# A new stored order for all tasks of a fused attention and ReGLU kernel on one core

## The chip, the cores and the metric

The kernel runs on one core of a Trainium2 chip. The metric is the device time of one execution in microseconds (us). PE stands for TensorE's matmuls and PEld for its weight loads, DVE for VectorE, ACT for ScalarE, POOL for GpSimd, and SP for SyncE, which only issues transfers here.

## The reference

Attention over 8 batches of 8 heads, 576 positions of 64 elements, with 16 beacon keys and values that every position sees ahead of the causal ones; then a feed-forward layer over all 8 x 576 = 4608 rows.

```python
k_all = concatenate([beacon_k, k]); v_all = concatenate([beacon_v, v])
scores = q @ k_all.T / 8, causal behind the 16 beacon columns
a = softmax(scores)
x = (a @ v_all), heads side by side      # 4608 x 512
out = (relu(x @ w_gate) * (x @ w_val)) @ w_out   # 512 -> 1536 -> 512
```

Inputs and the output are float32; the kernel computes in bfloat16 with float32 sums.

## The kernel before

The work of a batch is cut into small tasks. Loads bring a block of q, k or v in float32 into one of eight staging tiles `st`; a cast on POOL (some on DVE) rounds it to bfloat16 (L542 for q and k, L497 for v); PE transposes q and k blocks against an identity (L553, L626); ACT or DVE copies them out of PSUM into `qT` and `kT` (L493, L495). Score products (L824) go to PSUM, DVE adds the mask and takes the row minimum (L772), ACT takes the exponential with its sum (L779), DVE the reciprocal (L785), and POOL multiplies the row by it (L790). The results stand in `pb` (four tiles) and, for the last few positions of each head, in `pa` (two tiles). From batch 1 on a DMA transpose on SP's queue turns them into `pTb` and `pTa` (L910, 28 and 6 of them); for batch 0, and for one `pa` more, PE does this (L900). Products with v (L920 for `pTb`, L943 for `pTa`) give x, which is copied into the resident `xT`.

The feed-forward layer takes `xT` in ten spans of columns (240, 336, seven of 512, 448). For each of 12 hidden blocks PE makes four gate and four value matmuls (L981, L986), ACT applies the ReLU (L992), DVE multiplies (L997) into `hT`; then twelve matmuls for each 128 rows make the output (L1012), which is copied to one of three tiles `osb` and stored (L1026). All three weights stay in SBUF. PE fills its early waits with matmuls on the mask that nobody reads (L1064, "fillers").

The 2399 tasks are made in a fixed manner and numbered in the order in which they are made. A string `ORDER` (L77 on) lists them in the order in which their instructions are emitted; this order fixes each engine's instruction list, and SP's queue of transfers too. An entry is a task's number, with a letter where the engine is chosen (`a` ACT, `v` DVE, `g` POOL), and behind a colon the numbers of the tiles or PSUM banks that it takes. `f7:7` is a filler of seven matmuls on bank 7. Nothing is decided at run time: each engine goes through its list in order, and an instruction waits where data or a tile's previous use is not done. So a task that waits holds up all behind it on its engine, and a DMA transpose that waits for POOL holds up the loads and stores behind it on SP's queue.

```python
for t in plan.replay(ORDER):
    t.run(t)
```

The tasks that the prediction names, by number and the line of their work:

| tasks | engine | what |
|---|---|---|
| 431 | PE | scores, L824, batch 0 |
| 14.74 us row of L824 (469) | PE | scores, batch 0 |
| 1420, 1421, 1422 | POOL, SP, PE | the `pa` chain of one batch: L790, transpose L910, product L943 |
| 1282, 1279, 1306, 1305, 1294, 1316 | POOL | L790 on `pb`, other parts |
| 331, 338 | POOL | casts of loads, L542 |
| 1177 | SP | a `pTb` transpose, L910 |
| 1124, 1140, 1159, 1161, 1175 | POOL | L790 on `pb` |
| 285, 287 / 319 | POOL | casts of q, k loads, L542 / of a v load, L497 |
| 2065 | PE | a value group of four matmuls, L986 |

Of the kernel before, what the change touches and what calls it, by code (L numbers as in the profile page):

```python
# [80 lines left out]
420 59v:2 486:5.6.0.1 475 430 472 63v:0 454 473 438 487 64:2 453 435 60:7 464 69v 439 491 452 440:4 61a 72:0 476 495:3.1 13 73 441v:0 492 f3:7 455 465  # L81
496 488 444:0 467 f2:7 16 65v 504:4.5 497 77:1 489 500 442:2 445a:0 458 f3:7 505 457 f1:7 501 466 513:6.0 493 456 509 446:3 506 477 f1:7 f3:7 502 498
468 514 447a 443a 15 478:3 510 71v 482:4 518 522:1.2 515 19 511 524 479a:0 523:5.6 67g 516 519 483v:0 480:3 512 528 484:4 481a 18 525 548:7.3.2.3 485v
529 549 90:5 494 557:1.2 91 1734:4 553 17 550 1738:0 562 1735:0 566:5.6 507 503 1739:1 f2:7 558 563 1736:4 508 567 1742:7 559 490 1737:0 554 526 520
499 1740:4 571 1743:2 575:1.0 81:3 568 517 1741:1 82 1744:2 576 86:4 572 584:3.4 527 f1:7 580 1746:5 577 521 532:7 569 530 560 586 1747:1 531 536:1
533a:0 1748:5 1745:2 534:6 74:1.1 1749:3 537a 540:2 564 535v 587 78:2.1 95:0 544:5 542:1 541v:1 125:7 538:6 581 570 588 573 585:2.3 551 565 543a 555
539v 1750:0 561 545v 610:6.7.0 590 1751:1 552 546:4 589 578 611 591 1754:0 579 75:5 612 1752:1 1755:0 582 592 547v 76a 1756:3 574 613 1758:2 1757:5
593 594:4 1753:4 1759:0 596:5 556 595v:2 598:1 1762:0 583 614 79:7 597v 1760:4 1763:1 615 599a 602:2 1761:6 80a 606:5 87:1 616:1 604:4 617v:0 83:0
600:3 603v:3 92:2 101:3 84:6 601a 88:7 113:4 605v 607a 93:0 96:0 618:3 105:1 85a 89v 20 109:2 608:2 94a 99:6 97:5 126:1.0 609v 1766:1 98a 1764:4 619a
127:6 620:0.2.0.1 102:2 1765:7 128a 635:3.5 1770:7 1767:2 621 21 643 103:6 628 1768:4 622 1771:0 106:0 104a 1772:1 1769:8 624 1774:7 114:2 1773:9  # L90
1778:4 629 623 123:4 1776:1 1775:1 644 1779:2 1780:6 121:5 110:1 631 1792:4 1777:10 133:1 636 630 650:7.0 137:2 1781:11 1793:0 1787:2 637 129:0 645
646 659 107:6 652 639 111:4 1782:1 632 625 638 647 651 649 108a 112v 115:3 1788 633 653 640 116v 627 654 665:6.5 658 626 674:3.4 634 661 666 1794:7
642 660 670 1783 667 100:1 655 676 671 657 1784 119:6 124 677 700:0.6.2.3 1795:12 1785a:0 122 141:4 1796:5 701 679 117:3 668 656 708 715:7.1 702 678
648 1789 134:1 709 1797:1 704 669 717 145:1 1800:4 176:5 662 1790a:1 1798:3 716 664 723 703 1802:5 663 718 1799:13 641 1801:2 1804:2 724 1786 120 711
675:3.4 672 705 680 1803:14 149:6 1805:0 681 1806:0 726 683 682 1808:2 719 1807:15 673 690:3 1812:5 710 1809:1 712 130:0.0 730:6.0 684 725 1810:7 720
732 686 713 1814:1 738 1813:2 721 731 685 714 1816:5 1811:8 118 131:2 739 734 1818:4 687 1815:1 1817:1 689 745:3.7 733 1819:2 1820:1 688 741 735 746
754:5.6 132a 736 695:1 740 1822:4 750 722 1821:1 1824:0 757 142:0 747 1823:11 1828:1 151:7 707 751 756 755:3.4 138:2 1825:2 727 1832:2 742 748 758 737
763 1826:7 706 1829:0 752 749 1830:0 759 152 1827:4 728 691:1 760 764 693:7 762 692a 1831:5 765 761 780:5.6.1 694v 139:1 781 135:0 753 1833:1 770:2
143:3 766 1836:7 140v 146:1 136a 1834:2 782 729 1837:2 767 147:4 144a 1835:6 1838:0 769 783 148v 744 696:1 698:2 784 1839:10 790:5.6.0.1 785 805:4.7
1840:3 792 160:1 768 791 786:0 799 743 794 1841 177:2.1 775:3 798 697a 813 793 1842 150:0 787v:1 699a 814 801 153:0 788:2 807 800 178:1 1843a:2  # L100
820:0.5 789v 161:2 773:6 179a 828 815 806 771:2 1845:3 795 829 809 156:0 821 808 772v 1846 164:1 816 822 180:7 774v 831 835:2.4 1847 823 840 830 1791
824 817 1850:6 832 172:6 833 841 825 836 170:3 826 844:0.1 1848a:0 819 778:5 810 846 837 834 776:7 1851 811 777a 838 847 796 779a 157:1 154:2 849
845:4.5 184:0 165:0 848 1852 853 839 188:1 192:2 166:3 802 155v 1853a:1 804 162:0 1849 158:7 1855:1 854 812 174:5 850 167v 855 173 168:4 1857:6 163v
852 1856:2 159v 1859:2 827 856 797 857 1858:8 870:7.0.2.3 1860:1 851 885:4.3 1863:5 871 893 872 185:2 860:2 1867:2 886 874 878 842 894 843 1861:6 873
887 1864:2 858 896 1865:7 1862:9 803 1868:0 171 879 1871:5 895 859 888 875 1866:10 818 880 900:6.1 889 169 1869:2 865:1 909 881 175 901 1875:3 908
1872:1 189:0.1 1870:11 911 915:7.4 181:1 902 1873:2 910 890 916 904 892 903 182:1 876 1879:0 183v 193:1 1876:2 210:7 1874:4 917 861:6 863:3 196:2 897
882 862a 912 920 202:6 924:1.2 1880:0 200:1 925:6.7 927 921 1877:5 918 905 926 919 864a 226:0 1881:0 877 1878:13 928 933 914 950:3.4.0 929 868:5 206:5
906 1844 934 866:1 1883:2 930 224:4 867v 935 931 1882:14 1854 186:1 891 1884:1 190:6 187v 1887:0 203:0 191a 951 936 907 194:2 1885:6 932 195a 937 952
197:2 1888:2 940:2 1889:7 1886:15 953 899 869v 1895:1 938 954 1890:0 198:3 207:1 204:0 1891:4 199a 883 205v 884 959:6.5.7.2.0.1 1892:0 939 208:3 218:6
913 961 1893:4 898 209a 220:2 973 211:2 960 1899:0 965 1894:1 955 964 962 1897:3 974 956:0 1896:1 1900:2 963 1901:6 1898:2 967 230:5 941:0 975 943:4  # L110
# [56 lines left out]
2327 2334:12 2322 2351:7 2317 2328 2342:7 2338:13 2349:5 2348:1 2353:0 2329a:1 2343:2 2330 2318 2344:0 2352:2 2363:4 2319a:0 2354:1 2345:3 2320 2355:2  # L167
2346:5 2350:0 2323 2356:0 2364:2 2359:3 2365:0 2360:1 2324a:1 2357:2 2325 2367:7 2358:2 2361:3 2366:4 2368:0 2369:0 2371:4 2370:8 2373:2 2362:3 2372:1
2375:1 2374:10 2377:3 2376:2 2379:6 2378:9 2380 2384:0 2385 2381 2386 2382a:0 2389:5 2383 2387a:1 2388 2390 2391 2394:4.6 2392a:2 2393 2397:1 2395v:0
2398 2396  # L170
"""


# [924 lines left out]
```

## Time and profile before

| | |
|---|---|
| median of 3 runs | 400.01 us (399.12 to 400.79) |
| the profiled execution, its time | 399.52 us |
| the profiled execution, its span from first to last instruction | 397.6 us |
| granted PE clock over the span | 0.999 |
| HBM read, written | 38.54 MB, 9.44 MB |

A profile's page counts an engine's busy time as the union of its instructions; a PE that is busy need not be at its peak, since a matmul's start-to-start time is shorter than its duration. The chain is followed back from the last instruction, at each step to whatever released it. A releaser in square brackets, as in "[1.40 <-DMA pTa<-pa]", gives the idle time of that engine just before the row and what ended it. For a transfer the row of SP's queue is its issue; "DMA to landing" is the time from the issue to the last byte's arrival, as minimum, median and maximum.

### The profile page before, as it was taken

The page shows a single profiled execution, that of the slowest core. Times are in us where ns is not written, and L with a number is a line of the kernel's source. Part 1 is how long each engine was busy: PE and PEld are TensorE (multiplying, and loading weights), DVE is VectorE, ACT ScalarE, POOL GpSimd, SP SyncE. Part 2 cuts the span into 40 slices and gives each one's busy share as a digit, 9 for nine tenths or more (in the row PEclk, how much of TensorE's full clock was granted, in tenths as well). Part 3 has the DMA queues.
Part 4 walks back from the last instruction along what each step waited for, and adds up shares of the span by engine and source line. Part 5 has one row for each costly group of instructions (what it writes and reads, how often), then busy time and mean ns, then how long its engine had stood idle before and what let it go on. Part 6 is the DMA issues. An engine that isn't in the chain of part 4 may idle for free.

```text
span 397.6 us, 10026 instructions
## 1 busy us (share of the span) xinstructions
PE 380.1 (96%) x3384; PEld 199.7 (50%) x3428; DVE 274.2 (69%) x1008; ACT 270.3 (68%) x842; POOL 231.0 (58%) x447
## 2 busy tenths in 40 slices
PE   5789999999999999999999899999999999999996
PEld 3557855655454455454444454445444445444453
DVE  5899799888976888877876778567946832331230
ACT  1899699897877687789777789688746731332322
POOL 3799779959785789268827787663853650000000
PEclk9999999999999999999999999999999999999999
DMA  7999999999999999968997999988897556001102
GB/s 183 218 181 237 193 230 235 195 230 236 215 234 205 313 177 203 181 186 177 202 205 215 197 202 198 209 162 167 169 180 161 101 105 168 28 0 54 54 26 94
DMA packets 184100, 68.89 MB, mean 173 GB/s; under 512 B 158384, under 2 KB 179504, under 8 KB 184048
## 3 DMA queue, kind: packets, MB, share of 16 engines
q1 hardware_dynamic: 179216, 63.46, 74.5%
q0 software_dynamic: 4752, 4.72, 7.3%
q8 instruction: 27, 0.44, 0.5%
q14 instruction: 25, 0.20, 0.1%
q10 hardware_dynamic: 80, 0.07, 0.1%
HBM read 38.54 MB, written 9.44 MB: 121 GB/s over the span
## 4 chain that ended last, share of the span: by engine, by line
PE 83%; DMA 3%; issue 1%; DVE 1%; POOL 0%; ACT 0%; DVEq 0%
PE f L1012 22%; PE f L986 22%; PE f L981 22%; PE f L824 6%; PE f L920 6%; PE f L553 2%; DMA pTb<-pb 2%; DMA pTa<-pa 2%; PE f L943 1%; PE f L626 1%; PE f L874 1%; DVE f L772 0%; PE f L900 0%; POOL pa L790 0%; DVE kT L495 0%
## 5 line engine op out<-in xcount | busy, mean ns | idle before, releaser
L790 POOL TENSOR_SCALAR pb<-pb,small 128x384 bf16<-128x384 bf16 (+8 forms) x272 | 142.1, 538 | 45.5 <-DVE small L785 43.9
L779 ACT ACTIVATE pb<-f,small 128x448 bf16<-128x448 f32 (+8 forms) x272 | 144.8, 551 | 24.5 <-DVE small L772 19.7
L772 DVE CUSTOM_DVE_ANT_0 f<-f,mask 128x64 f32<-128x64 f32 (+8 forms) x288 | 136.3, 507 | 20.1 <-PE f L824 11.0
L997 DVE TENSOR_TENSOR hT<-g,f 128x512 bf16<-128x512 f32 (+3 forms) x120 | 74.4, 629 | 55.3 <-PE f L986 30.2
L981 PE MATMUL f<-xT,wg_r 128*128 128x512 bf16 (+3 forms) x466 | 108.1, 357 | 0.9 <-issue 0.2
L986 PE MATMUL f<-xT,wv_r 128*128 128x512 bf16 (+3 forms) x465 | 106.8, 357 | 1.2 <-issue 0.3
L1012 PE MATMUL f<-wo_r,hT 128*128 128x512 bf16 (+3 forms) x441 | 100.3, 374 | 1.5 <-issue 1.0
L992 ACT ACTIVATE g<-f 128x512 f32<-128x512 f32 (+3 forms) x120 | 65.8, 563 | 49.3 <-PE f L981 31.0
L981 PEld LDWEIGHTS <-wg_r 128*128 128x128 bf16 x480 | 45.0, 98 | 45.2 <-issue 2.5
L986 PEld LDWEIGHTS <-wv_r 128*128 128x128 bf16 x480 | 44.5, 98 | 44.2 <-issue 3.0
L1012 PEld LDWEIGHTS <-hT 128*128 128x128 bf16 (+3 forms) x456 | 41.9, 100 | 47.0 <-issue 2.9
L779 ACT ACTIVATION_READ_ACCUMULATOR pb<-f,small 128x1 f32 x272 | 60.0, 221 | 0.0
L542 POOL TENSOR_SCALAR h<-st 128x512 bf16<-128x512 f32 (+1 forms) x87 | 46.8, 547 | 22.5 <-DMA st<-in_q_dram 5.0
L772 DVE DVE_READ_ACCUMULATOR2_ANT small<- 128x1 f32 x296 | 41.2, 139 | 0.1
L824 PE MATMUL f<-kT,qT 64*64 64x64 bf16 (+7 forms) x640 | 34.6, 296 | 1.6 <-ACT pb L779 0.7
L497 POOL TENSOR_SCALAR v<-st 128x512 bf16<-128x512 f32 (+1 forms) x38 | 23.3, 616 | 19.7 <-DMA st<-in_v_dram 19.6
L493 ACT CAST xT<-f 128x240 bf16<-128x240 f32 (+2 forms) x46 | 16.1, 376 | 22.6 <-PE f L920 22.5
L785 DVE RECIPROCAL small<-small 128x2 f32<-128x2 f32 (+3 forms) x136 | 19.7, 160 | 12.0 <-ACT pb L779 10.8
L920 PE MATMUL f<-pTb,v 128*64 128x320 bf16 (+3 forms) x488 | 27.0, 254 | 0.4 <-DMA pTb<-pb 0.4
L824 PEld LDWEIGHTS <-qT 64*64 64x64 bf16 x640 | 14.7, 107 | 22.6 <-issue 17.7
L920 PEld LDWEIGHTS <-v 128*64 128x64 bf16 (+1 forms) x512 | 21.0, 109 | 9.9 <-issue 5.1
L553 PE MATMUL f<-ident,h 128*128 128x128 bf16 (+1 forms) x224 | 19.8, 222 | 5.7 <-DVE h L542 5.0
(62 smaller groups left out, 216.1 us busy)
## 6 DMA issues: line engine op xcount, KB each, us to landing
out_dram<-osb SPq DMA_DIRECT2D x34, 256.0 KB, 2.7
st<-in_k_dram SPq DMA_DIRECT2D x28, 256.0 KB, 4.6
st<-in_q_dram SPq DMA_DIRECT2D x28, 256.0 KB, 4.0
st<-in_v_dram SPq DMA_DIRECT2D x24, 256.0 KB, 4.6
st<-in_q_dram SPq DMA_DIRECT2D x16, 128.0 KB, 3.8
st<-in_k_dram SPq DMA_DIRECT2D x16, 128.0 KB, 4.1
st<-in_v_dram SPq DMA_DIRECT2D x8, 224.0 KB, 4.5
wv_r<-in_moe_w_val_dram POOLq DMA_DIRECT2D x3, 512.0 KB, 9.2
```

Of the source, the lines that this page charges most:

```text
L542: (nc.gpsimd if x.engine == "POOL" else nc.vector).tensor_scalar(to, src, by, 1.0, ALU.mult, ALU.mult)
L553: nc.tensor.matmul(to, h16.tile[:rows, a * P:(a + 1) * P], ident[:rows, :rows], start=True, stop=True)
L772: nc.vector.tensor_tensor_reduce(out=view(i, n - m), in0=view(i, n - m), in1=msk, scale=1.0, scalar=at(7) if m < n else 3.0e38, op0=ALU.ad ...
L779: nc.scalar.activation(ph.tile.rearrange("p a n -> p (a n)")[:, a:a + n], view(i), AF.Exp, bias=at(i), scale=-1.0, accum_out=at(4 + i))
L790: nc.gpsimd.tensor_scalar(one, one, at(8 + i), 1.0, ALU.mult, ALU.mult)
L824: nc.tensor.matmul(banks[k][b_].tile[64 * i:64 * i + 64, off:off + n], t.q.tile[r, 2 * g + i, 64 * j:64 * j + 64], t.kT.tile[r, 2 * g + i, ...
L920: nc.tensor.matmul(ps.tile[64 * hh:64 * hh + 64, d0:d0 + w], t.v.tile[:rows, c, D * h:D * h + D], rhs(64 * hh), start=(c == 0), stop=(c == ...
L981: nc.tensor.matmul(psg.tile[:, :mt], wg_r[:, ki, nf * P:(nf + 1) * P], xT[:, ki, m0:m0 + mt], start=(ki == 0), stop=(ki == KM - 1))
L986: nc.tensor.matmul(psv.tile[:, :mt], wv_r[:, ki, nf * P:(nf + 1) * P], xT[:, ki, m0:m0 + mt], start=(ki == 0), stop=(ki == KM - 1))
L992: r = add("ACT", c_act(mt), lambda _, psg=psg, g=g: nc.scalar.activation(g.tile[:, :mt], psg.tile[:, :mt], AF.Relu), (a,), (psg, g), -1000 ...
L997: hid.append(add("DVE", c_dve(mt), lambda _, psv=psv, g=g, nf=nf: nc.vector.tensor_mul(hT[nf].tile[:, :mt], g.tile[:, :mt], psv.tile[:, :m ...
L1012: nc.tensor.matmul(ps[c].tile[64 * c:64 * c + rows, :w], hT[nf].tile[:, t0:t0 + rows], wo_r[:, nf, w * c:w * c + w], start=(nf == 0), stop ...
```

## The change

Only the string `ORDER` differs. It holds the same 2399 tasks with another order, other tile and bank numbers, and another engine for 54 of the copies out of PSUM; its fillers are 13 entries with 43 matmuls in place of 14 with 46. The order on PE is much the same from about 30 us on: groups change places with neighbours. The orders on POOL, DVE and SP's queue change more. The head of the string, up to task 469:

```diff
-10 1 22:0 2 26:1 34:3 0 4 30:2 23v:0.0 8 38:4 24:0 9 5 f4:7 42:5 27g:1.0 7 25v 48:7 28:1 46:6 35v:0 31v:2 36:3 29v 32:2 50:0 f3:7 37v 33a 54:1 f2:7
-39v:1 410:4.5.0.0 58:2 11 431:6.0 6 40:1 411 43g:2 12 412 41a 423 44:2 413 45a 49g:0 422 3 436 414 448:3.1.0.0 62:7 415 421 f12:7 432 47g 426 68:5 450
-416 459 70:6 449 425 460 51g:0 451 469:2.4 424 66:4 f1:7 417 437 461 14 52:5 427 433 55v:1 470 53a 418 56:6 434 f8:7 474 428 463 419 57v 471 429 462
+11 4 22:0 3 2 26:1 34:3 0 5 1 30:2 f4:7 23v:0.0 9 38:4 8 12 24:0 42:5 27g:1.0 f2:7 48:7 28:1 35v:0 46:6 f2:7 6 29a 31v:2 f1:7 36:3 25v 32:2 50:0 f2:7
+37v 33a 39v:1 410:4.5.0.0 10 54:4 7 40:1 43g:2 411 423 58:2 413 41a 44:2 421 431:6.0 412 45a 49g:0 432 414 436 448:3.1.0.0 62:7 415 f7:7 422 416 47g
+68:5 460 424 451 469:2.4 425 70:6 461 51g:0 426 417 470 437 450 14 52:5 459 433 427 55v:1 53a 474 72:0 66:4 56:6 428 f3:7 449 464 429 434 57v 73 f7:7
...
```

Around transpose 1177, with the tasks on POOL that feed it (1124 to 1127, 1149 to 1151, 1168, 1169):

```diff
-1142 1123 1152 1972 1143 1266:0 1145 1144 1973 1146 1153 280:6 1147 1978 1974v:0 1155 1154 1981:3 1156 1975 1148 1979a:1 293:1 1162:0.1.5.6 1157 1980
-1096:7 1163 1098:4 318:2 1097a 1101:2 1158 1103:7 1170 1102a 1099a 1982 1136 1164 1104a 1140 1171 1166 1986:2 281:0.1 1165 1139 1267:4 1172 285:1
-282:1 1983 283v 1160 1268a 1167 1126 1187:7.0.4.5.2.3 1984a:2 1151 1995:1 1173 1189 1985 287:2 307:6 1201 1987 1188 1168 291:0 1190 1193 1203 300:7
-1125 1991:3 1191 1996:1 1127 1204 1192 1993:6 1194 1149 1202 1195 1150 1988 1174 1992:0 1169 1124 1205 1994:0 1999:7 1206 319:1 1177:3 1989v:0 1207
+1265 1977 1143 1124 271 1152 1972 1142 285:1 1146 1144 1973 287:2.1 1145 1153 1266:0 1147 1978 1154 1156 1981:3 1974v:0 1155 280:3 1157 1979v:1
+1162:0.1.5.6 1136 1096:7 291:0 1164 1101:2 1098:4 1097a 1158 1975 1171 1161 1103:7 1163 318:2 1099a 1982 307:6 1102v 1166 300:7 1170 281:0 1267:4 1165
+320:1 1148 1986:2 1127 1172 1167 1104v 1139 282:1 1268v 1173 1983 1160 283v 1168 1187:7.0.4.5.2.3 1984v:2 1149 1995:1 1125 1188 1985 1189 293:3 1169
+1991:3 1996:1 1174 1202 322:4 319:1 1192 1987 1175 1992:0 1201 1190 1193 1191 1993:6 1159 1150 1205 1204 1194 1988 1151 1206 1203 1994:0 1126 1195
+1999:7 1140 1177:3 1989v:0 1208 288:0.1 1196 1207 1214:3.2.4.6 2000:0 289v 294:1 1997:5 290a 1215 1216 2007:1 1209 1227 1218 1210 2003:0 1176 1219
```

Around the `pa` chain 1420, 1421, 1422 (316 and 337 are loads, 2048 and 1990 stores, 355 and 366 loads that come later in the new string):

```diff
-1416 1251:1 317 2040 1299 1254a 1252a 1417 1302 2041 1418 331:1 2046 327:0.0 1312 1317:0.1.5.6 2047a:2 1281 1313 1256:2 1319 1258:4 2042a:1 2048 1303
-1318 2054:3 1257a 1306 332:4 2043 1419 1325 1320 2049:7 337:0 339:2 1321 1326 328:2 2050 346:5 1291 1259v 1328 1294 1990 329v 315 1327 2055 355:6 1420
-1342:4.0.2.5.2.3 1314 1421:1 2063:6 1280 1343 1344 1304 2056 366:7 1316 2064:1 1357 353:3 1347 338:0 2051 1356 2057v:1 1360 1315 362:0 1348 2059:1
-1345 1305 1358 1361 1282 1322 2052v:0 2061:3 2060:0 1295 1359 1422:7 333:2 1346 2065:4 1323 2062:9 1349 1362 2067:2 1423v 1279 1363 1329 1324 2066:11
+1415:4.5.1 1253:0 330:5 1416 353:3 1251:1 2040 1309 337:0 1252a 1302 1254v 2041 1278 1417 1282 1418 2046 1281 2042v:1 1312 1317:0.1.5.6 2043 2047a:2
+1258:4 1313 1291 1303 1316 1318 1256:2 2054:3 315 1257a 1319 1326 2055 1320 1259v 338:0 1419 1325 1321 328:2 2049:7 331:1 329v 1327 1294 346:5 2050
+1279 332:4 1328 1306 1342:4.0.2.5.2.3 1305 2063:6 1343 1420 1356 1322 1344 2056 1323 1421:1 1347 1348 1324 2051 2057v:1 1280 362:0 1345 2059:1 1293
+1329 2052a:0 339:2 1357 2064:1 333:2 1346 2065:4 1361 1314 1359 1315 2061:3 1360 2060:0 1358 1304 1363 1422:7 1292 1332:0 2062:9 1350 2067:2 363:0
```

In the old string load 316 stands behind transpose 1255, in the new one ahead of transpose 1250, the one before it. The remaining lines of the string differ in the same manner.

More of the change, by code (lines that the diff above doesn't have):

```diff
@@ L82 @@
[L82 to L109, printed above, removed]
@@ new lines @@
+1843a:2 773:6 821 816 771:2 822 1845:3 809 828 156:5 179v 823 1846 164:1 808 829 1791 772a 774v 824 1847 172:6 815 825 180:7 830 835:2.4 817 795
+844:0.1 1848a:0 797 836 1850:6 831 153:0 840 837 1849 776:7 810 832 778:5 847 811 777a 157:1 841 154:2 846 1851 165:0 174:5 779a 848 170:3 158:7 812
+845:4.5 168:4 849 833 166:3 854 818 162:0 159a 1855:1 188:1 826 838 850 842 155a 853 827 1852 796 163v 1856:2 851 167a 1859:2 852 856 839 855 1857:1
+819 860:3 1860:1 857 885:4.3.2.3 1858:8 171 1853a:0 870:7.0 1867:2 872 843 1863:5 189:0.1 871 886 874 894 858 1861:6 887 873 1868:0 181:1 802 893
@@ L171 @@
+2350:0 2355:4 2324a:1 2353:0 2356:0 2352:2 2357:2 2354:1 2363:5 2359:3 2364:2 2367:7 2360:1 2319a:2 2365:0 2320 2361:3 2325 2366:4 2371:4 2362:3
+2369:0 2358:2 2372:1 2368:0 2373:2 2375:1 2374:10 2377:4 2370:8 2376:2 2379:6 2378:11 2384:0 2380 2381 2385 2382a:0 2383 2386 2389:5 2387a:1 2390 2388
+2391 2394:4.6 2392v:2 2393 2397:1 2395v:0 2398 2396
 """
```

122 lines of the change are left out of this document (71 added, 51 removed), and 6 rows, old and new, of the table ORDER.

## The prediction

> **What bounds the kernel now.** I read the page's span, busy times and chain first, then the busy time by stretch, then the waits one by one.
>
> ```profile
> span 397.6 us, 10026 instructions
> ...
> PE 380.1 (96%) x3384; PEld 199.7 (50%) x3428; DVE 274.2 (69%) x1008; ACT 270.3 (68%) x842; POOL 231.0 (58%) x447
> ...
> PE 83%; DMA 3%; issue 1%; DVE 1%; POOL 0%; ACT 0%; DVEq 0%
> ```
>
> PE is busy for 380.1 of 397.6 us and carries 83% of the chain, so at most 17.5 us can be won by any order, and only where PE stands still.
>
> ```profile
> 0.00:10.00 10.00, 5.33 (x45) 3.00 (x45) 5.75 (x42) 1.79 (x4) 3.60 (x15) 1.00 0.75 183
> 10.00:20.00 10.00, 7.91 (x75) 5.27 (x76) 8.96 (x51) 8.65 (x39) 8.00 (x17) 1.00 1.06 218
> 20.00:30.00 10.00, 8.56 (x100) 5.53 (x98) 10.00 (x38) 10.00 (x34) 9.88 (x20) 1.00 1.17 181
> ...
> 220.00:240.00 20.00, 18.44 (x218) 9.31 (x220) 16.12 (x55) 15.62 (x48) 15.91 (x31) 1.00 0.99 200
> ```
>
> The columns are the stretch, its length, the busy time of PE, PEld, DVE, ACT and POOL with their instructions, the granted clock, the DMA share and GB/s. In the first 30 us PE idles 4.67 + 2.09 + 1.44 = 8.2 us, and from 20 to 30 us DVE and ACT are full: there they bound the kernel, not PE. From 220 to 240 us PE loses 1.56 us. Two waits stand in the chain in order of time, both on a DMA transpose of softmax results:
>
> ```profile
> 112.50 7.62 DMA pTb<-pb
> ...
> 120.16 0.88 PE f L920 x16
> ...
> 215.53 6.25 DMA pTa<-pa
> ...
> 221.83 0.67 PE f L943 x20
> 222.50 0.87 PE f L986 x4
> ```
>
> PE's own idle before them is 0.4 us at 120.16 and 1.40 us at 221.83:
>
> ```profile
>   DMA pTb<-pb: 0.4, 1
> ```
>
> ```profile
> 221.83 0.67 PE L943 MATMUL f<-pTa,v 128*128 128x32 bf16 x20 [1.40 <-DMA pTa<-pa]
> ```
>
> So there are three prizes: the head, 0.4 us at 120, 1.4 us at 222. Everything else in this change can only keep PE fed or fail to.
>
> **The change, part by part.** The set of tasks stays the same; fillers go from 46 matmuls to 43, PE's instruction list from 6858 to 6852 rows, and 54 copies change engine (31 from ACT to DVE, 23 the other way).
>
> *Copies.* For the same 128x512 output copy:
>
> ```profile
> L493 ACT COPY osb<-f 128x512 f32<-128x512 f32 x24 | 14.0, 588 | 10.0 <-PE f L1012 9.8 <-ACT pb L779 0.2
> ...
> L495 DVE COPY osb<-f 128x512 f32<-128x512 f32 x10 | 6.9, 689 | 5.8 <-PE f L1012 4.5 <-DMA out_dram<-osb 1.3
> ```
>
> A net 8 copies on DVE cost some 8 x 0.1 = 0.8 us of engine time, hidden by the third of the span in which each of the two idles. If that cover were gone the whole 0.8 us would show; I take 0.
>
> *Head (tasks up to about 30 us).* Part of the constant and padding memsets move ahead of the first data, one 12-matmul filler becomes 7, and task 431 (a group of 256-column score products) moves behind two transposes.
>
> ```profile
> 9.03 0.25 DVE L463 MEMSET pb<- 128x32 uint32 x5
> ...
> 9.60 0.31 DVE L485 MEMSET xT<- 128x128 uint32 x2
> ...
> 11.05 0.43 DVE L772 CUSTOM_DVE_ANT_0 f<-f,mask 128x256 f32<-128x256 f32 x1
> ...
> 15.09 0.43 DVE L772 CUSTOM_DVE_ANT_0 f<-f,mask 128x256 f32<-128x256 f32 x1 [0.80 <-PE f L824]
> ```
>
> ```profile
> 12.06 2.74 PE L1064 MATMUL f<-mask,ident 128*128 128x256 bf16 x12
> 14.74 0.30 PE L824 MATMUL f<-kT,qT 64*64 64x256 bf16 x4
> ...
> 15.54 1.04 PE L1064 MATMUL f<-mask,ident 128*128 128x256 bf16 x8
> ```
>
> DVE is what the head waits for. On its list between 9 and 11.1 us stand memsets of about 0.6 us, of which about 0.3 stay behind: a gain of 0.3. Task 431's minima (the 11.05 row is one) can no longer start before about 11.3, since 431 now follows the second transpose, and DVE has then run out of other minima: I charge 0.5. The shorter filler (5 x 0.22 us less) lets the scores at 14.74 come about 1.1 us sooner, which removes most of DVE's 0.80 us wait at 15.09: a gain of 0.5. After that the two lists hold nearly the same DVE work up to 30 us. Sum -0.3; I take -0.2, with -1.1 (all of 0.3 and 0.80) and +0.5 (the loss alone) as ends. The three fewer fillers are inside this: they stand in time that DVE sets.
>
> Twelve fillers started over 2.68 us (12.06 to 14.74) and eight lasted 1.04, a spacing of 0.22 and about 0.11 us, though the granted clock reads 1.00 in this stretch. [...]
>
> *The wait at 222.* It is the chain of one task group: the normalisation of pa on POOL (task 1420, L790), its transpose on SP's queue (1421, L910), the product on PE (1422, L943). Three things move.
>
> ```profile
> 210.26 0.62 POOL L497 TENSOR_SCALAR v<-st 128x512 bf16<-128x512 f32 x1 [8.71 <-DMA st<-in_v_dram]
> ...
> 214.75 0.76 POOL L790 TENSOR_SCALAR pa<-pa,small 128x592 bf16<-128x592 bf16 x1
> ```
>
> ```profile
> 205.40 0.58 SPq L725 DMA_DIRECT2D st<-in_v_dram  x1
> ...
> 214.21 0.46 SPq L1026 DMA_DIRECT2D out_dram<-osb  x1
> 214.72 0.42 SPq L587 DMA_DIRECT2D st<-in_q_dram  x1
> 215.53 1.56 SPq L910 DMA_TRANSPOSE pTa<-pa  x1
> ```
>
> ```profile
> DMA to landing us min/median/max: 2.6/3.2/6.3
> ```
>
> ```profile
> L790 POOL TENSOR_SCALAR pb<-pb,small 128x384 bf16<-128x384 bf16 (+8 forms) x272 | 142.1, 538 | 45.5 <-DVE small L785 43.9
> ...
> L542 POOL TENSOR_SCALAR h<-st 128x512 bf16<-128x512 f32 (+1 forms) x87 | 46.8, 547 | 22.5 <-DMA st<-in_q_dram 5.0
> ...
> st<-in_k_dram SPq DMA_DIRECT2D x28, 256.0 KB, 4.6
> ```
>
> First, PE gets one more group of four matmuls (task 2065, the 222.50 row: 0.87 us) ahead of 1422. PE arrives 0.2 us sooner by the head, so 1422 is due at 221.83 - 1.40 + 0.87 - 0.2 = 221.1. Second, five tasks are put ahead of 1420 on POOL (1282, 1316, 1305 and 1279 of L790, 338 of L542): 4 x 0.54 + 0.55 = 2.7 us. But POOL had idled 8.71 us until 210.26 behind a v load, which is now fetched two transposes earlier, so 1282 and others can run in that idle time. What holds POOL instead is task 338: its load is the fourth after the transposes that end before 205.4, so it is issued near 205.4 + 3 x 0.6 = 207.2 and lands 4.6 us later, at 211.8. From there 338, 331, 1294, 1279, 1306, 1305 and 1420 need 6 x 0.54 + 0.76 = 4.0 us, which puts 1420's end near 215.8, 0.3 us later than now (214.75 + 0.76). Third, the SP queue: the store at 214.21 and the load at 214.72 leave from just ahead of the transpose, and this transpose took 6.25 us where the median of six is 3.2. With fewer transfers ahead I expect 3.2 to 6.3 us, so a landing at 219.0 to 222.1 against 221.1: the wait is between 0 and 1.0. I take 0.2, as the median is nearer to a calm queue: -1.2. Ends: -1.4, and +2.0 if POOL absorbs nothing (issue at 215.53 + 2.7 = 218.2, landing at 221.4 to 224.5, so 0.3 to 3.4 us of wait where 1.4 is now).
>
> The loads that leave from ahead of 1421 now stand behind the next two transposes; their products on PE come from 230 us on, so I charge nothing. If one were late it would cost what it is late, some tenths of a us.
>
> *A thin place made thinner, 188 us.*
>
> ```profile
> 172.27 0.58 POOL L790 TENSOR_SCALAR pb<-pb,small 128x384 bf16<-128x384 bf16 x1 [6.94 <-DVE small L785]
> ...
> 180.16 0.61 POOL L497 TENSOR_SCALAR v<-st 128x512 bf16<-128x512 f32 x1
> ```
>
> ```profile
> 180.22 3.78 SPq L910 DMA_TRANSPOSE pTb<-pb  x1
> ```
>
> ```profile
> 188.00 0.36 PE L920 MATMUL f<-pTb,v 128*64 128x128 bf16 x6
> ```
>
> ```profile
> DMA to landing us min/median/max: 5.6/6.4/8.1
> ```
>
> ```profile
> 180.00:190.00 10.00, 9.89 (x131) 4.72 (x131) 8.37 (x25) 8.89 (x28) 8.90 (x18) 1.00 0.85 168
> ```
>
> The transpose at 180.22 (task 1177) starts as the last of its POOL tasks ends and must land by 188.00; by the landings of its kind (5.6, 6.4, 8.1) it has 0 to 2.2 us to spare. In the new order 1175, 1161 and 1159 of L790 and 319 (the 180.16 row) stand ahead of its last POOL task, and 1140 (the 172.27 row) no longer does: 3 x 0.54 + 0.61 - 0.58 = +1.7 us. Against it, three tasks that were ready (1124 of L790, 285 and 287 of L542) now stand ahead of the one that waits, in POOL's 6.94 us of idle before 172.27: 0.54 + 2 x 0.55 = 1.6. So the transpose starts 0.1 to 1.7 us later, and PE comes 0.2 sooner. New wait: 0 to 1.9 us. I take 0.5, near the lower end, as PE idles only 0.11 us of these ten (9.89 busy): it is not late yet.
>
> *The wait at 120.* The transpose's place in the queue and PE's work ahead of it are unchanged; earlier PE only waits longer. 0, ends -0.4 and +0.3.
>
> *Rest.* From 30 us to the end most groups keep their place on PE to within a group or two, and each producer moves with its consumer. Taken as 0, ends -0.5 and +1.
>
> Sum: -0.2 - 1.2 + 0.5 = -0.9 us. The profiled execution took 399.52 us (1.9 outside its span), which gives 398.6; it lay 0.49 under the median of the runs shown, so I forecast **399.1 us** for the median.
>
> **Rivals.**
>
> *All three prizes are paid (faster).* Head -1.1, 120 us -0.4, 222 us -1.4, and no wait at 188: -2.9, 397.1 us. For it: DVE's and POOL's idle times above are real and the orders fill them. Against: in the head DVE and ACT are already full.
>
> *POOL's in-order queue (slower).* The new order hangs more work ahead of the normalisations that feed transposes. If POOL's idle time does not take it, because a load or reciprocal still blocks it, 222 us goes to +0.5 (the middle of 0.3 and 3.4, less 1.4), and 188 us to +1.9; with +0.5 from the rest and the head's -0.2 that is +2.7, 402.7 us. It decides from about 1 us of delay of either transpose on. For it: POOL waited 43.9 us in 24 places on exactly these reciprocals, up to 6.9 us.
>
> ```profile
> POOL pb L790 <- DVE small L785: 43.9, 24, 6.9
> ```
>
> [...]
>
> *Nothing moves.* The waits shift and add up to the same: 400.0 us.
>
> **How the numbers follow.** Forecast 0.35, faster rival 0.25, POOL queue 0.25, nothing 0.10, clock 0.05. A measurement of this kernel tells about 0.5%, 2 us, from no change: bounds 398.0 and 402.0. Faster is the first rival and a little of the forecast's edge, 0.26; slower is the POOL rival and as little, 0.26; the rest 0.48. The forecast's own range is 397.7 to 400.8 (the 222 us place from -1.4 to 0, the 188 us place from 0 to 1.2, the head from -0.2 to +0.3). Widened to both sides' rivals: 396.6 to 403.0.
>
> **What would show it.** PE's wait before L943 near 221 under 0.5 us; the pa transpose with about 3 us to landing, not 6; a new PE wait of about half a us on a pTb transpose near 187.5; PE's busy time from 20 to 30 us within 0.5 us of the 8.56 above. I am wrong if the head's PE work ends more than 1 us off, if the normalisation of pa comes 2 us later or more, or if a transpose that had room before (none of those above) makes PE wait over 1 us.

## The result, and the profile after

The new order takes 402.7 us (median of 20 runs, 399.16 to 405.26); the old one took 400.19 us beside it (20 runs, 398.43 to 402.12). The ratio is **1.0047, 95% interval 1.0027 to 1.0067**: slower by about half a per cent, some 1.9 us. A second set of runs of the same kernel, told below, gave 1.0066 (1.0040 to 1.0092). (The ratio is that of the fast runs, which leaves out one run of the new order, of 405.26 us; the two medians by themselves give 1.0063, inside the interval.) The profiled execution took 402.79 us.

The page of the new kernel, its span, busy times and chain:

```profile
span 400.9 us, 10056 instructions
...
PE 385.1 (96%) x3425; PEld 200.7 (50%) x3425; DVE 280.7 (70%) x1013; ACT 270.4 (67%) x837; POOL 231.7 (58%) x447
...
PE 78%; DMA 8%; ACT 5%; DVE 3%; POOL 2%; SPq 1%; issue 1%; POOLq 0%; DVEq 0%
```

PE's sum is no measure here, as the trace of before holds only 3384 records of matmuls for its 3428 weight loads, that of the new kernel all 3425. The chain tells more: transfers went from 3% to 8% of it. The busy time by stretch shows where, first of the new kernel, then of the old (columns as in the prediction):

```profile
50.00:60.00 10.00, 9.29 (x79) 5.17 (x77) 8.96 (x39) 8.92 (x31) 5.42 (x12) 1.00 1.07 208
...
80.00:100.00 20.00, 18.62 (x176) 9.76 (x175) 13.79 (x60) 16.09 (x55) 12.61 (x26) 1.00 0.96 209
100.00:120.00 20.00, 17.30 (x146) 8.75 (x144) 15.03 (x54) 15.23 (x47) 13.62 (x27) 1.00 1.11 226
...
220.00:240.00 20.00, 19.99 (x215) 9.60 (x218) 15.95 (x54) 16.43 (x52) 12.77 (x25) 1.00 0.94 188
```

```profile
50.00:60.00 10.00, 9.95 (x88) 5.46 (x88) 9.34 (x42) 9.36 (x35) 7.67 (x15) 1.00 1.22 229
...
80.00:100.00 20.00, 19.89 (x183) 10.26 (x186) 17.32 (x71) 16.96 (x60) 14.58 (x29) 1.00 1.02 235
100.00:120.00 20.00, 19.49 (x169) 9.73 (x172) 17.27 (x61) 16.70 (x51) 15.05 (x29) 1.00 1.15 224
```

PE now stands still for 0.7 + 1.4 + 2.7 us between 50 and 120 us, where it lost 0.05 + 0.1 + 0.5; and from 220 to 240 us, where it lost 1.56, nothing is lost any more. Four waits make the loss. PE's timeline of the new kernel, with the idle time and its releaser in brackets:

```profile
57.42 1.02 PE L1012 MATMUL f<-wo_r,hT 128*128 128x512 bf16 x4 [0.71 <-DMA wo_r<-in_moe_w_out_dram]
...
92.19 0.40 PE L553 MATMUL f<-ident,h 128*128 128x128 bf16 x4 [1.38 <-POOL h L542]
...
111.17 0.88 PE L920 MATMUL f<-pTb,v 128*64 128x320 bf16 x16 [0.95 <-DMA pTb<-pb]
...
119.12 0.40 PE L553 MATMUL f<-ident,h 128*128 128x128 bf16 x4 [1.75 <-POOL h L542]
```

These are output group 1784, turn 158 (a turn is the transposition of a block of q or k on PE, L553), values 868 (a product with v) and turn 204. (Counted from when the group would have started at the usual start-to-start time, they cost some 0.89, 1.55, 1.03 and 1.91 us; most waits told below are in that measure, those in brackets are idle times.) What stands ahead of three of them in the chain is a transfer, of the third and last block of output weights, of q and of k:

```profile
47.70 9.67 DMA wo_r<-in_moe_w_out_dram
...
85.95 5.49 DMA st<-in_q_dram
...
112.11 6.18 DMA st<-in_k_dram
```

To compare kernels I use three marks at which all the orders have done the same PE tasks: A is value group 1740, B value group 1897, C value group 2105 (all L986). Old, then new:

```profile
30.16 0.57 PE L986 MATMUL f<-xT,wv_r 128*128 128x240 bf16 x4 [0.15 <-DVE hT L997]
...
117.92 1.24 PE L986 MATMUL f<-xT,wv_r 128*128 128x512 bf16 x5
...
244.62 0.38 PE L986 MATMUL f<-xT,wv_r 128*128 128x512 bf16 x1
```

```profile
30.15 0.57 PE L986 MATMUL f<-xT,wv_r 128*128 128x240 bf16 x4
...
122.84 1.24 PE L986 MATMUL f<-xT,wv_r 128*128 128x512 bf16 x5
...
247.91 1.03 PE L986 MATMUL f<-xT,wv_r 128*128 128x512 bf16 x4
```

From A to B the old order takes 87.76 us, the new one 92.69: 4.9 lost. From B to C it is 126.70 and 125.07: 1.6 won (in the table below the last digit can differ, as the rows are rounded). The head up to A and the stretch behind C (153.0 in both) are the same. So the sum +3.3 is the difference of the spans, 400.9 - 397.6.

### The profile page after: what moved, and what is told of

The parts are those of the page before. It is cut to its first block, busy times and chain, and to the rows that moved or that the text cites. A ratio compares the mean times of both kernels' runs of the same rounds, so it can differ in the third digit from the quotient of the medians.

```text
span 400.9 us, 10056 instructions
## 1 busy us (share of the span) xinstructions
PE 385.1 (96%) x3425; PEld 200.7 (50%) x3425; DVE 280.7 (70%) x1013; ACT 270.4 (67%) x837; POOL 231.7 (58%) x447
## 4 chain that ended last, share of the span: by engine, by line
PE 78%; DMA 8%; ACT 5%; DVE 3%; POOL 2%; SPq 1%; issue 1%; POOLq 0%; DVEq 0%
PE f L981 20%; PE f L986 20%; PE f L1012 20%; PE f L824 5%; PE f L920 5%; ACT pb L779 4%; PE f L553 2%; DMA wo_r<-in_moe_w_out_dram 2%; DMA pTb<-pb 2%; POOL pb L790 2%; DMA st<-in_k_dram 2%; DMA st<-in_q_dram 1%; PE f L900 1%; PE f L943 1%; PE f L1064 1%
## 5 line engine op out<-in xcount | busy, mean ns | idle before, releaser
L790 POOL TENSOR_SCALAR pb<-pb,small 128x512 bf16<-128x512 bf16 (+8 forms) x272 | 142.9, 546 | 62.9 <-DVE small L785 49.7
L772 DVE CUSTOM_DVE_ANT_0 f<-f,mask 128x192 f32<-128x192 f32 (+8 forms) x288 | 136.7, 508 | 22.7 <-PE f L824 14.2
L986 PE MATMUL f<-xT,wv_r 128*128 128x512 bf16 (+3 forms) x480 | 107.2, 358 | 0.0
L1012 PE MATMUL f<-wo_r,hT 128*128 128x512 bf16 (+3 forms) x456 | 102.7, 374 | 0.8 <-DMA wo_r<-in_moe_w_out_dram 0.7
L986 PEld LDWEIGHTS <-wv_r 128*128 128x128 bf16 x480 | 44.9, 98 | 44.7 <-issue 2.3
L779 ACT ACTIVATION_READ_ACCUMULATOR pb<-f,small 128x1 f32 x272 | 58.8, 216 | 0.0
L553 PE MATMUL f<-ident,h 128*128 128x128 bf16 (+1 forms) x224 | 21.0, 229 | 4.8 <-POOL h L542 3.6
L493 ACT CAST xT<-f 128x320 bf16<-128x320 f32 (+2 forms) x39 | 14.9, 390 | 15.3 <-PE f L920 15.0
```

The source lines that it names most:

```text
L553: nc.tensor.matmul(to, h16.tile[:rows, a * P:(a + 1) * P], ident[:rows, :rows], start=True, stop=True)
L772: nc.vector.tensor_tensor_reduce(out=view(i, n - m), in0=view(i, n - m), in1=msk, scale=1.0, scalar=at(7) if m < n else 3.0e38, op0=ALU.ad ...
L779: nc.scalar.activation(ph.tile.rearrange("p a n -> p (a n)")[:, a:a + n], view(i), AF.Exp, bias=at(i), scale=-1.0, accum_out=at(4 + i))
L790: nc.gpsimd.tensor_scalar(one, one, at(8 + i), 1.0, ALU.mult, ALU.mult)
L986: nc.tensor.matmul(psv.tile[:, :mt], wv_r[:, ki, nf * P:(nf + 1) * P], xT[:, ki, m0:m0 + mt], start=(ki == 0), stop=(ki == KM - 1))
L1012: nc.tensor.matmul(ps[c].tile[64 * c:64 * c + rows, :w], hT[nf].tile[:, t0:t0 + rows], wo_r[:, nf, w * c:w * c + w], start=(nf == 0), stop ...
```

## The experiments

All ratios are to the old kernel, with 95% intervals; A to B and B to C are of the one profiled execution.

| run | ratio | A to B, us | B to C, us |
|---|---|---|---|
| old order | 1 | 87.76 | 126.71 |
| new order | 1.0047 (1.0027 to 1.0067) | 92.69 | 125.06 |
| after_again | 1.0066 (1.0040 to 1.0092) | 92.43 | 125.07 |
| u92 | 1.0074 (1.0048 to 1.0100) | 92.69 | 125.06 |
| u119 | 1.0018 (0.9992 to 1.0043) | 90.27 | 125.70 |
| u_late | 1.0011 (0.9985 to 1.0037) | 91.04 | 125.06 |
| u_all | 1.0022 (0.9990 to 1.0054) | 89.09 | 126.82 |
| u_all2 | 1.0010 (0.9981 to 1.0039) | 89.73 | 125.06 |
| s_ba | 1.0018 (0.9993 to 1.0044) | 89.86 | 126.57 |
| s_ab | 1.0143 (1.0107 to 1.0179) | 93.06 | 127.49 |
| s_ba2 | 1.0017 (0.9996 to 1.0037) | 89.39 | 125.68 |
| h_sp | 1.0495 (1.0472 to 1.0519) | 99.25 | 136.30 |
| h_pool | 1.0140 (1.0109 to 1.0170) | 94.04 | 128.62 |
| h_pe | 1.0061 (1.0042 to 1.0081) | 92.41 | 126.24 |
| l_before | 0.9959 (0.9934 to 0.9984) | 88.51 | 125.02 |
| l_after | 0.9955 (0.9936 to 0.9975) | 88.00 | 125.08 |
| h5 | 1.0018 (0.9997 to 1.0040) | 92.70 | 125.06 |
| b222 | 1.0026 (1.0005 to 1.0047) | 89.71 | 128.22 |
| b222b | 0.9984 (0.9958 to 1.0011) | 88.77 | 126.61 |

**One place undone at a time.** My first theory was four single places, each with its own price.

u92, PE's and ACT's lists around turn 158:

```diff
 PE
-154 1851 158 845 166 162 1855 1852 1859
+154 1851 845 1852 1855 158 166 162 1859
 ACT
-848 849 159 155 1856
+848 849 155 1856 159
```

> The new order with one place put back: the q turn (task 158) that waited 1.55 us at 92.19 now stands behind two output and gate groups and two copies changed places on ACT. Theory (four single places, each its own price): the wait at 92 goes, the later ones (1.03 us at 111, 1.91 us at 119) stay within 0.4 us, so the time falls by 1.5 us against the new order, ratio to before 1.001 where the new order has 1.0047. Rival (SP's queue and POOL deliver late as a whole between 85 and 120 us, and PE only waits for them in one place or another): PE comes 1.5 us sooner to the next late delivery, the waits at 111 and 119 grow by 1.5 us together, and the ratio stays near 1.0047.

The wait at 92 went, and nothing was won: A to B is 92.69 us as before. PE's timeline of this run shows where the time went:

```profile
96.49 0.41 PE L824 MATMUL f<-kT,qT 64*64 64x128 bf16 x8 [0.50 <-ACT pb L779]
...
111.14 0.60 PE L920 MATMUL f<-pTb,v 128*64 128x320 bf16 x6 [1.44 <-DMA pTb<-pb]
...
119.75 0.40 PE L553 MATMUL f<-ident,h 128*128 128x128 bf16 x4 [2.15 <-POOL h L542]
```

A new wait at 96 and longer ones at 111 and 119. That is the rival, late as a whole.

u119, SP's queue:

```diff
-865 206 224 242 196 210 1844 202 200 940
+865 196 202 206 224 242 210 1844 200 940
```

> The new order with the k loads 196 and 202 put ahead of 206, 224 and 242 on SP's queue, straight behind transpose 865. Theory of single places: load 202 is issued near 108.5 us and not 112.1, lands near 114.5, the turn 204 does not wait any more, and the time falls by 1.9 us: ratio to before 1.000. The waits at 57, 92 and 111 stay. Rival (late as a whole): the loads that now stand behind, 206, 224 and 242, or transpose 940 behind them, come too late instead and cost about the same in new waits up to 130 us: ratio 1.004.

(196 is a load of q, not of k. Where the order of the loads asks for it, this run and the three below hand out staging tiles anew.) Load 202 left at 109.38 us, the wait at 119 went, A to B fell by 2.4 us to 90.27, and a new wait of 0.7 us came at 122.96 behind transpose 940. Not all of the 2.4 us is the edit's: the wait at 92 was absent in this execution too, and that of 1784 was 1.62 us, both ahead of the edit. The ratio is in between the two expectations; its interval meets those of the new order.

u_late is u119 with two places more:

```diff
 POOL
-843 189 858 181 834 803 804 876 859
+843 858 834 803 804 859 181 189 876
 SP
-860 184 1854 192 865 206 224 242 196 210 1844 202 200 940
+860 184 192 865 196 202 1854 206 224 242 210 1844 200 940
```

> The new order with the places at 111 and 119 put back: on POOL three tasks that transpose 865 does not need (181, 189, 876) go behind its last normalisation 859, on SP's queue store 1854 goes behind 865, and loads 196 and 202 follow 865. Theory of single places: 865 is issued near 102.4 us and not 103.3, both waits go, the time falls by 2.9 us against the new order: ratio to before 0.9975. Rival (late as a whole): what was put behind comes late, gain under 1 us, ratio over 1.002.

1.0011: no more than u119 within the intervals. Idle times of 1.65 us at 58.5, 1.09 at 93.7 and 0.68 at 111.6 stand in its profile.

u_all is u_late with u92's edit and, on PE, `674 1794 1783 1784` in place of `674 1783 1784 1794`.

> The new order with all four places put back (at 57 us a value group ahead of the first output group that needs the second block of output weights; at 92, 111 and 119 as in the other runs). Theory of single places: 5.4 us of waits go and the gains of the new order at 120 and 222 us stay: 402.79 - 5.4 = 397.4 us beside a profile of 399.5 before, ratio 0.992 to 0.995, faster than both. Rival (late as a whole): PE, 5 us sooner, meets the transposes of 110 to 130 us and the loads there before they have landed; at least half comes back as new waits, ratio 1.000 or more. Rival (something spread over all of PE's work, as a slower clock): no single wait explains it, ratio stays over 1.003 though the waits are gone.

A to B came down to 89.09 us, so the 3.6 us lost there (worked out below) are back; but the ratio is 1.0022, and not the 0.992 to 0.995 of the theory. Of its new waits the longest stands just behind B:

```profile
122.20 0.49 PE L920 MATMUL f<-pTb,v 128*64 128x128 bf16 x8 [1.69 <-DMA pTb<-pb]
```

```profile
111.86 10.30 DMA pTb<-pb
```

This is product 941 behind transpose 940 (the row of the chain): the wait at 120 of the old order, 1.69 us where it was 0.4. PE comes 4.2 us sooner to B than in the new order, but the transpose lands at 122.2 where it did at 121.9 (114.27 + 7.6).

u_all2 puts that transpose first:

```diff
-865 196 202 1854 206 224 242 210 1844 200 940 222
+865 196 202 1854 206 224 210 940 200 1844 242 222
```

> The new order with all four places put back (u_all) and, against the wait of 1.85 us that then stood at 122 us behind transpose 940, this transpose put ahead of load 242, store 1844 and load 200 on SP's queue. If the wait at 122 came from the bytes ahead of the transpose in a full stream: 940 is issued near 110.5 and not 111.9 us, lands near 119 us, the wait shrinks below 0.5 us, and the time falls by 1.3 to 1.8 us against u_all: ratio to before 0.998 to 0.999. If the supply is late as a whole: loads 200 and 242 come late instead, a new wait of 1 us or more stands between 122 and 135 us, ratio 1.001 to 1.003.

The transpose was issued at 112.00 us, no sooner, but its time to landing fell from 10.3 us to

```profile
DMA to landing us min/median/max: 7.8/7.8/7.8
```

The wait at 122 is gone, and B to C is 125.06 us with no new wait up to C. The shorter landing fits the bytes ahead. That it ended the wait is not shown: PE also came 1.8 us later (mark B at 120.44 us against 118.62 in u_all), which by itself is more than the wait of 1.69. The ratio, 1.0010, cannot be told from that of u_all, nor from 1.

**The two halves of the order.** The tasks of one order up to a point, then the rest as the other order has it: s_ba old up to about 126 us, then new; s_ab the other way; s_ba2 old up to about 205 us, then new.

> The old order up to about 126 us (its first 985 entries), the new order for all tasks after that. Theory (all of the loss lies before 126 us, the gain at 222 us is real and its own): no waits but those of before up to 126, the 0.5 us at 120 among them, and no wait of 1.57 us at 222: ratio to before 0.996, span 396.0 to 396.5 us. Rival (the wait at 222 went only because PE came there some 3 to 4 us late): with PE on time the wait comes back, ratio 1.000.

> The new order up to about 126 us (its first 985 entries), the old order for all tasks after that. If the new order loses before 126 us and gains at 222: the loss without the gain, ratio 1.008 or more, with the wait of 1 to 1.6 us at 222 back. If the two halves do not add up that way (landings differ from one execution to the next by as much): ratio near 1.005 or less.

> The old order up to about 205 us (its first 1500 entries), the new order after that, so that the seam lies where no turn waits. Theory: no loss from the stretch of 46 to 126 us, the gain at 222, ratio 0.996 to 0.998. Rival (the second half of the new order gains nothing, and the loss is not confined to the first half): ratio 1.000 to 1.002 as with the seam at 126.

s_ab is as expected: the new order's loss (93.06) with the old order's wait at 222 (1.02 us). s_ba and s_ba2 have no wait at 222, yet neither is faster than before. Up to 126 us s_ba is the old order entry by entry, and waits there as the profile of before does not:

```profile
55.11 0.40 PE L553 MATMUL f<-ident,h 128*128 128x128 bf16 x4 [1.74 <-POOL h L542]
```

So the profile of before is a good one of its kind. Five kernels carry the old order from A to B (old, s_ba, s_ba2, b222, b222b): 87.76 to 89.86, mean 89.10 us. Three carry the new one (new, after_again, s_ab): 92.43 to 93.06, mean 92.73. The loss is then **3.6 us**, not 4.9. s_ba also has a wait of 0.91 us at the seam (132.70) and one of 1.32 at 292.78, which the new order's profile lacks.

**The same kernel again.**

> The new order once more, unchanged, for a second profile and as measure in the same session. If the four waits at 57, 92, 111 and 119 belong to the order: all four are there again, within 0.5 us each, ratio 1.003 to 1.0065. If they are chance of one execution: at least two are gone and others stand elsewhere, while the ratio is the same.

The waits at 57 and 92 were not there. Those at the end of the stretch were:

```profile
109.14 0.46 PE L920 MATMUL f<-pTb,v 128*64 128x320 bf16 x4 [1.02 <-DMA pTb<-pb]
...
117.48 0.34 PE L553 MATMUL f<-ident,h 128*128 128x128 bf16 x3 [2.04 <-POOL h L542]
```

Right behind the second one PE loses some 1.4 us more, up to 120.5, but not by waiting: it is busy all the time, while the granted clock is halved (0.51 in its column):

```profile
117.70:121.20 3.50, 3.50 (x29) 1.39 (x26) 1.66 (x8) 1.14 (x3) 0.98 (x3) 0.51 1.04 236
```

With that, A to B is 92.43. So PE is late at B by nearly the same amount, though it waits less. s_ab has such a stretch too, 0.51 from 93.6 to 97.1 us, right behind a wait of 1.52 us on turn 166. Two of the three figures from A to B of the new order thus hold a stretch of half clock, which its first profile and the five of the old order do not.

**One engine's list alone.** The old kernel with the list of one engine taken from the new order between about 46 and 127 us: SP's queue (h_sp), POOL (h_pool) or PE (h_pe). Staging tiles are handed out anew where the order asks for it.

> The old kernel with nothing but the order of SP's queue taken from the new one, between about 46 and 127 us (the lists of PE, ACT, DVE and POOL stay as they are). If the loss comes from the order of the transfers alone: waits of 3 us or more between 85 and 125 us, ratio 1.008. If SP's order does no harm without the new lists of POOL or PE: ratio within 1.002.

> The old kernel with nothing but POOL's list taken from the new one, between about 46 and 127 us. If the loss comes from POOL's in-order list (tasks put ahead of the normalisations that the transposes wait for): the transposes near 97 and 102 us are issued 1 us late or more, PE waits 1 us or more behind them, ratio 1.004 or more. If not: within 1.002.

> The old kernel with nothing but PE's list taken from the new one, between about 46 and 127 us. If the loss comes from PE's groups changing places (turns ahead of their loads): a wait of 0.5 to 1.5 us near 91 us on turn 158, and one near 57 us on the output weights, ratio 1.003 to 1.006. If the turns are not late without the new transfer order: within 1.002.

All three are slower, h_sp by 5% with a wait of 6 us on turn 182 at 112. h_pool's ratio is as expected, but its waits are not behind the transposes named: the longest, 2.52 us, is on turn 131 at 70.35. h_pe loses as much from A to B as the whole new order (92.41 us), also at other places than expected: 1.44 us on turn 111 at 54.38, where s_ba, in the old order, waits 1.74; 0.61 on ACT at 89.71; nothing on turn 158 or on the output weights. Each list was made for the other engines' lists, so these runs do not share out the loss of the new order among the engines. They show what a mismatch costs; that PE's new list by itself makes the loss is not ruled out.

**Fewer bytes.** From the third batch on most loads bring half of the partitions (the last batch's q and k, and the loads put together from two tensors, stay whole):

```diff
-nc.sync.dma_start(st.tile.rearrange("p (h e) -> p h e", h=2),
+nc.sync.dma_start(st.tile.rearrange("p (h e) -> p h e", h=2)[:64 if b > 1 else P],
...
-nc.sync.dma_start(s3[:rows], heads(v, b, P * c - Nb, rows))
+nc.sync.dma_start(s3[:rows if b < 2 else rows // 2], heads(v, b, P * c - Nb, rows if b < 2 else rows // 2))
```

> The old order, but from the third batch on the loads of q, k and v bring only half of their partitions (the casts then work on old data in the other half, so the output is not the reference's; every other instruction stays). If landings are late because the 16 DMA engines are full between 50 and 260 us: fewer bytes let PE wait nowhere but in the head, the wait of 1.57 us at 222 and that at 120 shrink, span about 395.5 to 396 us, ratio to before 0.995. If the late work is made by POOL, DVE and the order of SP's queue: no change, ratio 0.998 to 1.001.

> The new order with the same half loads. If the new order's loss is landing time under full DMA engines: its four waits shrink below 0.3 us each, and it is level with the old order with half loads or 0.3 to 0.5 us faster (less filler work): ratio to before 0.994 to 0.995. If the loss lies in POOL's and SP's in-order lists (transposes held up by normalisations): the waits at 111 and 119 stay, and it stays 1.5 to 2 us behind the old order with half loads.

Both orders are level, 0.9959 and 0.9955. In the new order with half loads PE loses nothing from 80 to 120 us; this is its busy time by stretch, and below it the row of the DMA engines' busy tenths, of the whole loads and of the half ones, both in the new order:

```profile
80.00:100.00 20.00, 20.00 (x183) 10.52 (x182) 15.18 (x69) 17.29 (x59) 14.25 (x29) 1.00 0.82 180
100.00:120.00 20.00, 20.00 (x175) 10.14 (x174) 17.11 (x60) 17.58 (x55) 15.06 (x29) 1.00 0.94 192
```

```profile
DMA  7999899998998999898996899989889454100012
```

```profile
DMA  7999998896997686958793799987899453100012
```

With whole loads the 16 engines are busy in eight tenths and more of nearly every slice up to 310 us. POOL's, DVE's and SP's lists are the same in l_after as in the new kernel, so it is not these alone that hold PE up: the loss needs the bytes as well. Whether by full engines or because a half load itself lands sooner is not told apart: the DMA share is still 0.94 from 100 to 120 us, where PE waits for nothing. In l_before the wait at 222 is gone too, with the old order there.

In h5 only five loads are halved, those ahead of load 202 on SP's queue, by the same edit with `n0 in (196, 206, 210, 224, 242)`, n0 being the task's number.

> The new order with half of the partitions left out in five loads only, 206, 224, 242, 196 and 210: those that stand on SP's queue between transpose 865 and load 202, on which the turn at 119 us waits. (The casts take old data there; the output is not the reference's.) Load 202 itself is whole. If 204 waits because five whole loads are ahead of its load in a full stream (0.6 MB less at about 230 GB/s, 2.7 us): the wait of 1.9 to 2.2 us at 119 shrinks below 0.5 us, ratio 1.001 to 1.003. If it waits because staging tiles and POOL hold the queue up: the wait stays over 1.5 us and the ratio at 1.0047 to 1.0066.

The wait at 119 went and the ratio fell to 1.0018, as expected. But the profiled execution (402.94 us, over its median of 402.09) has the same A to B, 92.70, because of longer waits ahead of it:

```profile
58.04 0.38 PE L1012 MATMUL f<-wo_r,hT 128*128 128x512 bf16 x1 [1.08 <-DMA wo_r<-in_moe_w_out_dram]
...
94.42 0.34 PE L553 MATMUL f<-ident,h 128*128 128x128 bf16 x3 [1.73 <-POOL h L542]
...
113.35 0.46 PE L920 MATMUL f<-pTb,v 128*64 128x320 bf16 x4 [1.71 <-DMA pTb<-pb]
```

The profile and the ratio do not agree, so this run leaves open how much of the wait at 119 is bytes.

**The place at 222 by itself,** in the old order:

```diff
 SP, b222
-346 1990 355 1421 366
+346 1421 355 1990 366
 SP, b222b
-346 1990 355 1421 366
+346 1990 1421 355 366
 PE, both
-1422 2065
+2065 1422
```

> The old order with only the place at 222 us changed as the new order has it: on SP's queue store 1990 and load 355 go from ahead of transpose 1421 to behind it, and on PE the value group 2065 goes ahead of product 1422. Theory (this term of the prediction was right and stands by itself): the wait of 1.57 us at 222 is gone, nothing else changes, ratio to before 0.996 to 0.998. Rival (the gain needs the rest of the new order, as the splice at 126 us seems to say): some wait comes back between 222 and 260 us, ratio 0.999 to 1.001.

The transpose's landing fell to 3.0 us, yet product 1422 waited, for something else:

```profile
224.78 0.38 PE L943 MATMUL f<-pTa,v 128*128 128x32 bf16 x9 [0.56 <-DVE osb L495]
```

It needs PSUM bank 7, which copy 2052 frees; the copy needs the output tile that store 1990 empties, and the edit puts that store behind the transpose. The expectation says that the new order has it so, which holds for load 355 only: there it is issued far behind the transpose, at 239.60 us, but store 1990 far ahead of it, at 197.20. DVE's timeline shows the copy:

```profile
224.04 0.69 DVE L495 COPY osb<-f 128x512 f32<-128x512 f32 x1 [2.01 <-DMA out_dram<-osb]
```

Turn 334 waited 0.85 us besides, and turn 244, which is ahead of the place and not touched, 1.27 us at 144.22, where the profile of before has no wait.

> The old order with two of the three moves at 222 us: load 355 behind transpose 1421, value group 2065 ahead of product 1422; store 1990 stays ahead of the transpose. In b222 the transpose landed in 3.0 us, but 1422 still waited 0.6 us for a PSUM bank, whose copy by DVE waited for an output tile that the later store gave free. If that was what ate the gain: no wait on L943 over 0.3 us, no more late bank, ratio to before 0.997 to 0.999. If one load fewer ahead is not enough: landing still 5 to 6 us, wait 0.3 to 0.7 us, ratio 0.999 to 1.002.

With the store left in place there is no wait before L943 and no late bank; the transpose took this long:

```profile
DMA to landing us min/median/max: 4.6/4.6/4.6
```

But from B to C nothing is won in this profile (126.61 us against 126.71), as turn 244 waited here as well:

```profile
144.84 0.62 PE L553 MATMUL f<-ident,h 128*128 128x128 bf16 x8 [1.04 <-POOL h L542]
```

The interval of the ratio, 0.9958 to 1.0011, holds both a gain of 1.4 us and none. None of the versions with whole loads is shown to be faster than the old order.

## Why the prediction was wrong

**The step that failed is "Rest. ... each producer moves with its consumer. Taken as 0, ends -0.5 and +1."** Between A and B this term was +3.6 us (mean of three profiles against five); with the 1.6 us won from B to C that makes 2.0, near the 1.9 of the ratio. Producers did not move with their consumers: load 202 fell behind five entries of SP's queue and was issued at 112.11 us instead of 106.39, 5.7 us later, while PE came to its turn 3.0 us later by the waits before. This is known of the cause:

- It is not one wait but several, most of them on transfers that come late. Taking away the wait at 92 (u92) left A to B at 92.69 us; putting two loads ahead on SP's queue (u119) brought it to 90.27; all four places undone (u_all, u_all2) brought it to 89.09 and 89.73, inside the old order's range (one profile each).
- It needs the bytes of whole loads: with half loads the new order takes 88.00 us from A to B, and the old one 88.51. That this is because the DMA engines are full is argued, not shown.
- In two of the three profiles a stretch with a granted clock of 0.51 over 3.5 us is part of it; at that clock it costs up to 1.7 us (an estimate, 0.49 of 3.5).
- It is not shown how much of it each of the lists of POOL, SP and PE makes.

The last block of the output weights starts from POOL's queue, and 1784 waited for its landing, which took 9.67 us (47.70 to 57.37) while SP's loads ran too and the DMA share was 1.14; in the old order it took 9.4 us, from an issue 0.6 us sooner. How much of these times the loads of SP's queue make is not shown.

**The head** was put at -0.2 us; mark A stands at 30.15 against 30.16. That is right within what A differs between runs of the old order (29.74 to 31.48; the last in b222b, whose granted clock was 0.51 from 27.0 to 30.5 us), but partly by luck, for the faster spacing of matmuls (0.11 us where it was 0.22) came late, a case that stands in the forecast's chances as "clock", with 0.05. The old order's eight fillers at 15.54 us took 1.04 us; ten in the new order's profile, still 0.21 us apart, took 2.34, and the next three, at 21.06 us, took 0.50, 0.11 apart:

```profile
15.09 2.34 PE L1064 MATMUL f<-mask,ident 128*128 128x256 bf16 x10
...
21.06 0.50 PE L1064 MATMUL f<-mask,ident 128*128 128x256 bf16 x3
```

In nine of the ten profiles with the new head the ten are as slow. In the tenth, u_all, the same ten were fast, and A stands at 29.54 us, where the nine have 30.15 to 30.79:

```profile
15.01 1.25 PE L1064 MATMUL f<-mask,ident 128*128 128x256 bf16 x10
```

So the late spacing costs some 0.6 to 1.3 us here (an estimate, one profile against nine), and the rest of the new head seems to win about as much. What brings the faster spacing on is not shown.

**The wait at 222** was put at -1.2 us, and in every profile with the new order there it is gone: B to C is 125.06 us in most. The landing of its transpose, which I put at 3.2 to 6.3 us, is shorter still:

```profile
DMA to landing us min/median/max: 2.6/2.6/2.6
```

On the way two sizes were wrong and cancelled, by luck. Task 1420 ended at 221.69 us, 6.2 us later than before (215.51), of which PE's own lag just ahead of the place is 4.4 (group 2063 at 220.60 against 216.16 us); so it came about 1.8 us late and not the 0.3 that I worked out from POOL's idle time. The transpose, issued at 221.72, still landed 1.5 us ahead of PE (225.79).

**The thin place at 188** was put at +0.5 us. Its transpose was issued at 184.41, 4.2 us later than before, and PE came 4.7 us later: no wait. In u_all and u_all2, where PE is on time at B, there is none either. The term is 0.

**The wait at 120** was put at 0. In the new order it is gone because PE is late there: its transpose landed at 121.86 us, 1.7 us later than before, and PE came 4.5 us later. Where PE is on time (u_all, with other loads ahead of the transpose) it is 1.69 us.

**The rivals.** The POOL rival gave 402.7 us, the measured median, but by other places: 222 and 188 us, where nothing was lost. Only the wait at 111 is of its kind: transpose 865 was issued at 103.33, just behind its last normalisation. The list of what would make the prediction wrong had the right sign: "a transpose that had room before makes PE wait over 1 us" is values 868, with 1.03 us. It did not name loads, which cost more. Another of its signs came too, the normalisation of pa 2 us later or more, but most of its 6.2 us is PE's own lag.

**A sum.** The forecast's own range is added up wrongly: its ends, -1.6 and +1.5 us around no change, give 398.4 to 401.5 and not 397.7 to 400.8.

## What to carry to other kernels

Where an order is replaced as a whole, do not price only the waits that the old profile shows. List every load and transpose by the change of its place in the issuing queue against the change of its consumer's place; an entry that falls back five places, as load 202 did, can be a new wait (1.91 us here). A wait taken away from PE is time won only if PE's next transfers have landed by then (in u92 the wait at 92 us went, and A to B stayed at 92.69 us), so compare the time between two marks, not the wait, and read the granted clock between them, which can lose as much as a wait (some 1.4 us in after_again, at 0.51). And an early store can be worth more than it looks, if a tile and a PSUM bank hang on it (in b222 PE waited 0.56 us behind the later store).

## What was not expected of the hardware

Two executions of the new kernel put their waits in different places and still came to mark B at nearly the same time, 92.69 and 92.43 us from A; u92 and h5, with four waits each at other places or of other lengths, took 92.69 and 92.70. Why they agree so closely was not settled.

In after_again and s_ab the granted clock was 0.51 over 3.5 us right behind waits of 2.04 and 1.52 us (idle times), and h_pool, whose mean clock was 0.995, has such a stretch behind one of 2.52 us; behind one of 2.15 us in u92 (mean clock 0.999) there was none. A mean clock below 0.997 is more frequent in the new order: 11 of its 32 executions have one, 14 of 133 of the old order's. How much of the ratio this makes was not settled.

The same `pa` transpose landed 6.3, 5.7 (s_ab) and 5.3 us (h_pe) after its issue with the old neighbours on SP's queue, and 2.6 with the new ones. The `pTb` transpose 940 took 7.62 us in the old order and 10.30 in u_all, issued within 0.7 us of the same time.
